# Last products of an inverse Fourier step: 128 channels as weights in two row halves instead of 64 in four quarters of the array

## The chip, the cores and the metric

The kernel runs on one core of one Trainium2 chip. The metric is the device time of one execution in microseconds (us). Three runs of the kernel before gave 2576.21, 2576.61 and 2581.67 us; the median, 2576.61 us, is the time before.

## What is computed

The reference filters each of 8 sequences of 3008 tokens and 256 channels in the frequency domain and passes the result through a two-layer network with SiLU. Everything is fp32.

```python
X = np.fft.rfft(x, axis=1)                       # x: 8 x 3008 x 256
Y = X * (filt_r + 1j * filt_i)[None]             # filters: 1505 x 256
y = np.fft.irfft(Y, n=3008, axis=1).reshape(24064, 256)
h = y @ w_in                                     # 256 x 2048
out = (h / (1 + np.exp(-h))) @ w_out             # 2048 x 256
```

## The kernel before

**The network.** The tokens are worked in 48 pairs of blocks (`PAIRS`, six for each sequence), and the 2048 hidden units in 8 steps for each pair, so there are 384 steps. Each step does 7 products for the hidden layer (`hidden`, line 758) and 7 for the output layer (`project`, line 821); seven rather than eight, because the 2 x 2 blocks are multiplied by a scheme that saves one product and pays with additions on VectorE. All of them use weights of 128 x 128 and 256 or 240 moving columns. The TensorE instructions of a step are written out one after the other by Python generators; `hidden` of one step and `project` of the step before are interleaved by rounds, 8 to a step.

**The Fourier part.** 3008 is split as 47 x 64. For each sequence `b`, `spectral(b)` does forward products, the multiplication with the filter and the inverse, and its pieces stand between the matmuls of the network steps of the sequence before. Where each piece goes is written by hand: `put(step, round, piece)`, `open_step` and `join` add it to the list `pending`, and `until` takes from it between rounds. The order of the instructions on every engine is therefore fixed in the program; no scheduler changes it. Sequence 0 has nothing to hide behind and is worked at the start, in the first 75 us.

**The last inverse products, `stage3(g)`, lines 576 to 602.** There are 8 groups `g` for each of 8 sequences, so 64 calls. A tile `t4` holds the values of 4 time residues `i` and 256 channels; its partitions 0 to 47 belong to half `h = 0` and 64 to 111 to half `h = 1` (48 rows: 24 frequency residues, real and imaginary parts). For each `h`, `i` and channel, the 48 values are multiplied with a constant table `wi_t` of 48 x 47, which gives 47 time points. In the instruction `t4` is the weights (`lhsT`, so the result has channels on its partitions) and `wi_t` streams as 47 moving columns. The two halves `h` use the upper and lower 64 rows of the array and write two PSUM banks, `ps[0]` and `ps[1]`, called `pd` in the profile. The channels come in blocks of 128 (`cb`), and each block in two parts of 64 (`c0`), which use the left and right 64 columns of the array. So four matmuls, two `c0` by two `h`, stand on four different quarters of the array. A call issues 2 (`cb`) x 4 (`i`) x 2 (`c0`) x 2 (`h`) = 32 matmuls. Each fp32 matmul appears in the profile as two weight loads and two matmul passes, so a call has 64 of each.

**Around it.** `load_t4` brings the `t4` tile of two groups later on SyncE's queue. After the products `evict_y` (line 608; line 602 for the first four calls) copies `ps[0]` and `ps[1]` into the tile `y` that the network reads, one copy on ScalarE and one on VectorE. A piece that has just `alone` uses the banks of `px` and `pyz`, one under `join` uses those of accumulators, so the products wait until the last reader of these banks is done. The first four calls (sequence 0, `g` 0 to 3) stand in the start phase beside VectorE's work that prepares the network's weights (lines 973 to 988).

Of the kernel before, what the change touches and what calls it, by code (L numbers as in the profile page):

```python
# [56 lines left out]
NS, NG = 24, 6  # L57
# [113 lines left out]
def kernel(  # L171
# [9 lines left out]
    nc = tc.nc  # L181
# [41 lines left out]
    wi_t = cpool.tile([128, N1], FP32)  # L223
# [27 lines left out]
    def bank(b, name, spare=None):  # L251


        if early[0] is None and spare in ("x", "yz"):
            return xps.tile([128, 2, C], FP32, name=name, tag=spare)
        if early[0] is None and spare is not None:
            return accps.tile([128, 2, C], FP32, name=name, tag=f"a{spare}")
        if early[0] is None:
            return fps.tile([128, 2, C], FP32, name=name, tag="f")
        early[0] += 1  # L260
        k = early[0] % 8
        if k < 2:
            return fps.tile([128, 2, C], FP32, name=name, tag="f")
        if k > 5:
            return xps.tile([128, 2, C], FP32, name=name, tag="x" if k == 6 else "yz")
        return accps.tile([128, 2, C], FP32, name=name, tag=f"a{k - 2}")

    def spectral(b):
# [295 lines left out]
        def load_t4(g):  # L564
            t4s[g] = t4pool.tile([128, 4, C], FP32, name=f"t4_{b}_{g}", tag="t4")
            for h in range(2):
                nc.sync.dma_start(out=t4s[g][64 * h:64 * h + 2 * NS], in_=d2[:, 4 * g:4 * g + 4, h, :])
# [8 lines left out]
        def stage3(g, home=None):  # L576

            half, n0 = divmod(4 * g, 16)
            ps = [bank(b, f"pd_{b}_{g}_{h}", home[h] if home else None)
                  .rearrange("p a c -> p (a c)")[:, 0:8 * N1]  # L580
                  .rearrange("p (a i n) -> p a i n", a=2, i=4) for h in range(2)]
            t4 = us["t4"][:, 4 * g:4 * g + 4] if b == 0 and g < 4 else t4s[g]
            for cb in range(2):
                for i in range(4):
                    for c0 in (0, 64):
                        for h in range(2):
                            rows = slice(64 * h, 64 * h + 2 * NS)
                            nc.tensor.matmul(  # L588
                                out=ps[h][c0:c0 + 64, cb, i, :],
                                lhsT=t4[rows, i, 128 * cb + c0:128 * cb + c0 + 64],  # L590
                                rhs=wi_t[rows, :], start=True, stop=True)
            if g < 6 and (b > 0 or g > 3):
                load_t4(g + 2)
            if n0 == 0:
                y[b, half] = ypool.tile([128, 2, HALF], FP32, name=f"y_{b}_{half}", tag="y")
            if early[0] is None:
                us["pd", g] = ps
                return
            dst = y[b, half].rearrange("p a (r h n) -> p a h r n", h=2, n=16)
            for h in range(2):  # L600
                copy = nc.vector.tensor_copy if g > 1 and h == 1 else nc.scalar.copy
                copy(out=dst[:, :, h, :, n0:n0 + 4], in_=ps[h].rearrange("p a i n -> p a n i"))  # L602

        def evict_y(g, h):
# [5 lines left out]
        return dict(us=us, store_rows=store_rows, evict_y=evict_y, evict_t1=evict_t1, halves=halves, load_first=load_first, stage1_first=stage1_first, fill_first=fill_first, load_x=load_x, load_two=load_two, sums=sums, stage1=stage1, reverse_x=reverse_x,  # L610
                    load_fold=load_fold, fold=fold, stage1_fold=stage1_fold, evict_fold=evict_fold,
                    load_t2=load_t2, forward=forward, multiply=multiply, add=add, inverse=inverse, inverse_first=inverse_first, rows_first=rows_first, even=even, rows=rows, load_t4=load_t4, load_t4_rows=load_t4_rows, stage3=stage3)

    pending = []
# [637 lines left out]
```

## Time and profile before

| what | value |
|---|---|
| median of 3 runs | 2576.61 us (2576.21 to 2581.67) |
| span of the profiled execution | 2574.2 us, 2.4 us less than the median of the runs |
| TensorE matmul (PE) | busy 2550.8 us (99%), 18810 passes |
| TensorE weight load (PEld) | busy 2195.8 us (85%), 18810 loads |
| VectorE (DVE), ScalarE (ACT), GpSimd (POOL) | 65%, 42%, 17% |
| mean granted TensorE clock | 0.997 |
| line 588, 60 calls after the start | 3840 passes, busy 67.2 us; 3840 loads, busy 61.2 us |
| line 588, the 4 calls in the start | 256 passes, busy 4.5 us; 256 loads, busy 4.2 us |

In the rows of the profile a group is given as line, engine, operation, output <- inputs, rows x columns of the array in use, shape of the operand, count; then the time in which at least one of the group was in flight, the mean duration of one, and the idle time before it. Passes and loads overlap in time, so a count times a mean is far more than the busy time. What a stage costs is read from the starts in the timeline, not from the means. A row of the timeline is a run of instructions of one line: its start, the time from the first start to the last end, and the number.

### The profile page before, as it was taken

What the parts mean: (1) busy time and instruction counts of PE and PEld (TensorE: products, weight loads), DVE (VectorE), ACT (ScalarE), POOL (GpSimd) and SP (SyncE); (2) the same over time, 40 slices, a digit from 0 to 9 for tenths busy, and PEclk for the clock granted to TensorE, in tenths of its full rate; (3) what the DMA queues carried; (4) which work ended last, traced back from release to release, by engine and by line L of the source; (5) the groups of instructions that cost most, each with busy time, mean ns of one, the idle gap of its engine ahead of it and who ended that gap; (6) DMA issues with size and microseconds to landing.
All of it is one profiled execution on the core that took longest, in us unless ns stands there. A gap on an engine that the chain in (4) does not pass through costs nothing.

```text
span 2574.2 us, 48031 instructions
## 1 busy us (share of the span) xinstructions
PE 2550.8 (99%) x18810; PEld 2195.8 (85%) x18810; DVE 1665.8 (65%) x3591; ACT 1086.3 (42%) x3009; POOL 429.1 (17%) x685
## 2 busy tenths in 40 slices
PE   8999999999999999999999999999999999999998
PEld 6688888888888888888888888888888888888987
DVE  7866666676666666666666676666666666555554
ACT  3544444444444444444444444444444444444443
POOL 3212111211121111311121111211121112101101
PEclk9999999999999999999999999999999999999999
DMA  9522232222222222322223122331232211200011
GB/s 290 160 60 53 78 70 64 60 73 67 59 64 68 73 67 50 82 70 67 58 73 78 48 67 63 76 79 46 66 85 67 67 42 33 60 18 16 9 17 17
DMA packets 199611, 171.08 MB, mean 66 GB/s; under 512 B 122068, under 2 KB 173380, under 8 KB 198500
## 3 DMA queue, kind: packets, MB, share of 16 engines
q1 hardware_dynamic: 178392, 117.06, 19.7%
q0 software_dynamic: 17344, 45.70, 5.6%
q10 hardware_dynamic: 3648, 5.24, 0.7%
q8 instruction: 148, 2.42, 0.4%
q14 instruction: 79, 0.65, 0.1%
HBM read 96.07 MB, written 81.26 MB: 69 GB/s over the span
## 4 chain that ended last, share of the span: by engine, by line
PE 96%; DMA 1%; DVE 1%; issue 0%; ACT 0%; POOL 0%; SPq 0%; DVEq 0%; ACTq 0%
PE acc L821 44%; PE px L758 26%; PE pyz L758 19%; PE pd L588 2%; PE pb L467 2%; PE pc L510 2%; PE pf L434 1%; PE pc L530 0%; DMA filt<-in_filt_i_dram 0%; PE pa L354 0%; DMA w_t<-in_x_dram 0%; PE pa L345 0%; DMA d_t<-d_tbl 0%; DVE w_t L988 0%; DMA raw<-in_moe_w_in_dram 0%
## 5 line engine op out<-in xcount | busy, mean ns | idle before, releaser
L821 PE MATMUL acc<-g,w_t 128*128 128x256 f32 (+1 forms) x5376 | 1510.2, 375 | 0.4 <-DVE g L729 0.4
L821 PEld LDWEIGHTS acc<-g,w_t 128*128 128x128 f32 x5376 | 1023.0, 190 | 114.4 <-DVE g L729 0.8
L729 DVE TENSOR_TENSOR g<-pyz,abc 128x256 f32<-128x256 f32 (+1 forms) x1152 | 480.1, 417 | 620.1 <-ACT abc L779 356.6
L729 DVE TENSOR_TENSOR g<-g 128x256 f32<-128x256 f32 (+3 forms) x1152 | 599.7, 521 | 196.7 <-ACT g L762 183.5
L758 PE MATMUL px<-ty,w_t 128*128 128x256 f32 (+1 forms) x2304 | 679.1, 376 | 1.8 <-ACT abc L773 1.2
L762 ACT ACTIVATE g<-g 128x256 f32<-128x256 f32 (+1 forms) x1152 | 472.9, 411 | 250.7 <-DVE g L729 250.7
L729 POOL TENSOR_TENSOR s<-s 128x256 f32<-128x256 f32 (+1 forms) x329 | 254.9, 792 | 1417.8 <-DVE s L841 1289.7
L758 PEld LDWEIGHTS px<-ty,w_t 128*128 128x128 f32 x2304 | 432.7, 190 | 65.3 <-issue 6.2
L758 PE MATMUL pyz<-y,w_t 128*128 128x256 f32 (+1 forms) x1536 | 454.1, 377 | 0.0
L758 PEld LDWEIGHTS pyz<-y,w_t 128*128 128x128 f32 x1536 | 283.8, 190 | 47.6 <-DVE g L729 7.7
L773 ACT COPY abc<-px 128x256 f32<-128x256 f32 (+1 forms) x384 | 141.2, 368 | 372.7 <-PE px L758 372.7
L779 ACT COPY abc<-px 128x256 f32<-128x256 f32 (+1 forms) x384 | 141.5, 368 | 338.1 <-PE px L758 337.1
L762 ACT ACTIVATE g<-px 128x256 f32<-128x256 f32 (+1 forms) x384 | 145.8, 380 | 300.9 <-PE px L758 300.7
L758 PE MATMUL px<-y,w_t 128*128 128x256 f32 (+1 forms) x768 | 232.3, 384 | 1.0 <-DVE y L602 1.0
L758 PE MATMUL pyz<-ty,w_t 128*128 128x256 f32 (+1 forms) x768 | 225.4, 375 | 0.2 <-DVE g L729 0.2
L758 PEld LDWEIGHTS px<-y,w_t 128*128 128x128 f32 x768 | 140.5, 190 | 32.9 <-DVE y L608 5.8
L758 PEld LDWEIGHTS pyz<-ty,w_t 128*128 128x128 f32 x768 | 144.5, 190 | 18.7 <-DVE g L729 1.0
L766 ACT COPY abc<-px 128x256 f32<-128x256 f32 (+1 forms) x384 | 135.3, 352 | 52.3 <-PE px L758 52.3
L588 PEld LDWEIGHTS pd<-wi_t,t 48*64 48x64 f32 x3840 | 61.2, 135 | 25.3 <-ACT g L762 16.4
L446 POOL DMA_DIRECT2D d<-tf x144 | 71.6, 504 | 29.5 <-DVE tf L442 29.5
L871 DVE STREAM_TRANSPOSE o<-s 128x256 f32<-128x256 f32 x192 | 74.0, 423 | 0.4 <-issue 0.4
L841 ACT COPY s<-acc 128x512 f32<-128x512 f32 (+1 forms) x94 | 54.2, 577 | 47.6 <-PE acc L821 47.3
(137 smaller groups left out, 1264.4 us busy)
## 6 DMA issues: line engine op xcount, KB each, us to landing
t<-d SPq DMA_DIRECT2D x120, 192.0 KB
t<-d SPq DMA_DIRECT2D x84, 256.0 KB
d<-q POOLq DMA_DIRECT2D x84, 256.0 KB, 2.7
out_dram<-o SPq DMA_DIRECT2D x636, 32.0 KB
d<-tf POOLq DMA_DIRECT2D x144, 96.0 KB, 3.5
xr<-in_x_dram SPq DMA_DIRECT2D x6, 1472.0 KB
x_all<-in_x_dram SPq DMA_DIRECT2D x72, 96.0 KB
x_all<-xr SPq DMA_DIRECT2D x72, 96.0 KB
```

Source lines behind the costliest of these rows:

```text
L446: nc.gpsimd.dma_start(out=d1[k // 2, :, k % 2, n0:n0 + 4], in_=us["tf"][32 * k:32 * k + NS].rearrange("p q n c -> p (q n) c"))
L467: nc.tensor.matmul(out=ps[k][32 * j:32 * j + 32, ri, :], lhsT=d_t[rows, 4 * g + at, ri, :], rhs=rhs, start=True, stop=True)
L588: nc.tensor.matmul(out=ps[h][c0:c0 + 64, cb, i, :], lhsT=t4[rows, i, 128 * cb + c0:128 * cb + c0 + 64], rhs=wi_t[rows, :], start=True, sto ...
L729: eng.tensor_tensor(out=out, in0=in0, in1=in1, op=op)
L758: nc.tensor.matmul(out=out, lhsT=w_t[:, jp, c, 0], rhs=rhs, start=start, stop=True, skip_group_check=True)
L762: nc.scalar.activation(out=g[:, k, 0:n], in_=g[:, k, 0:n] if src is None else src, func=AFT.Silu)
L766: nc.scalar.copy(out=sums[:, 0, 0:n], in_=xo)
L773: nc.scalar.copy(out=sums[:, 1, 0:n], in_=xo)
L779: nc.scalar.copy(out=sums[:, 2, 0:n], in_=xo)
L821: nc.tensor.matmul(out=acc[pair][i][:, h, 0:n], lhsT=w_t[:, jp, c, 1], rhs=g[:, k, 0:n], start=(jp == 0 and h == 0), stop=last, skip_group ...
L841: copy(out=s[:, 2 * i:2 * i + 2, 0:n], in_=acc[pair][i][:, :, 0:n])
L871: v.transpose(out=o[:, :, h, :], in_=results[pair][:, ((2, 6), (4, 1))[chunk][h], :])
```

## The change

The loop over `c0` goes away. Each matmul takes a whole block of 128 channels as its weights and writes 128 partitions of PSUM; the halves `h` stay on the upper and lower rows of the array. A call issues 16 matmuls instead of 32, so 32 passes and 32 loads instead of 64 and 64, two at a time instead of four. The moving operand (47 columns of `wi_t`), the banks, the results and their places are the same. In the built program the waits stand on the same places (the first matmul of each half), and the instruction order on every engine is otherwise unchanged.

```diff
             for cb in range(2):
                 for i in range(4):
-                    for c0 in (0, 64):
-                        for h in range(2):
-                            rows = slice(64 * h, 64 * h + 2 * NS)
-                            nc.tensor.matmul(
-                                out=ps[h][c0:c0 + 64, cb, i, :],
-                                lhsT=t4[rows, i, 128 * cb + c0:128 * cb + c0 + 64],
-                                rhs=wi_t[rows, :], start=True, stop=True)
+                    for h in range(2):
+                        rows = slice(64 * h, 64 * h + 2 * NS)
+                        nc.tensor.matmul(out=ps[h][:, cb, i, :], lhsT=t4[rows, i, 128 * cb:128 * cb + 128],
+                                         rhs=wi_t[rows, :], start=True, stop=True)
```

## The prediction, made before the changed kernel ran

> **What bounds the kernel now.** I read the page's first part (busy times) and its fourth (the chain that ended last) before anything else.
>
> ```profile
> PE 2550.8 (99%) x18810; PEld 2195.8 (85%) x18810; DVE 1665.8 (65%) x3591; ACT 1086.3 (42%) x3009; POOL 429.1 (17%) x685
> ...
> PE 96%; DMA 1%; DVE 1%; issue 0%; ACT 0%; POOL 0%; SPq 0%; DVEq 0%; ACTq 0%
> ```
>
> TensorE is busy for 99% of the span and 96% of the chain is its work. So a stage of TensorE that gets longer or shorter moves the end by the same amount, unless TensorE waits soon after it for something else. The view of waits, asked for TensorE's matmuls alone, lists fourteen waits of together about 14 us in 2574, nearly all of them before 85 us. From 85 us on there is next to nothing that could swallow added time.
>
> Next, the groups of weight loads, different shapes kept apart; the last two numbers that matter are the mean duration of one load (after the comma) and, before it, the busy time.
>
> ```profile
> L821 PEld LDWEIGHTS acc<-g,w_t 128*128 128x128 f32 x5376 | 1023.0, 190 | 114.4 <-DVE g L729 0.8
> ...
> L588 PEld LDWEIGHTS pd<-wi_t,t 48*64 48x64 f32 x3840 | 61.2, 135 | 25.3 <-ACT g L762 16.4 <-issue 8.5 <-DVE g L729 0.4
> L510 PEld LDWEIGHTS pc<-z,e_t 32*64 32x64 f32 x1344 | 28.3, 131 | 10.6 <-PE acc L821 6.8
> L467 PEld LDWEIGHTS pb<-t,d_t 64*32 64x32 f32 x1344 | 20.5, 106 | 15.4 <-issue 7.1 <-PE px L758 2.3
> ```
>
> A load's duration goes with its columns (128: 190 ns, 64: 131 to 135, 32: 106), about 0.9 ns for each, and hardly with its rows (32 or 48 rows, 131 or 135). From 64 to 128 columns it is 55 ns. That is a latency; what a load keeps others waiting is read from starts. Here is the timeline of the loads around one call of the changed stage, and then around two calls in a row.
>
> ```profile
> 152.74 0.41 PEld L821 LDWEIGHTS acc<-g,w_t 128*128 128x128 f32 x2
> 153.48 1.02 PEld L588 LDWEIGHTS pd<-wi_t,t 48*64 48x64 f32 x64 [0.33 <-issue]
> 154.56 0.30 PEld L758 LDWEIGHTS px<-ty,w_t 128*128 128x128 f32 x2
> 154.88 0.41 PEld L821 LDWEIGHTS acc<-g,w_t 128*128 128x128 f32 x2
> ```
>
> ```profile
> 335.26 1.96 PEld L588 LDWEIGHTS pd<-wi_t,t 48*64 48x64 f32 x128 [0.33 <-issue]
> 337.27 0.30 PEld L758 LDWEIGHTS px<-y,w_t 128*128 128x128 f32 x2
> ```
>
> Three readings. **(1) The pace now.** 128 loads are 32 rounds of four quarters. From the first start to the last end it is 1.96 us; less the last load (0.135) and the three starts inside a round (0.02), 31 rounds take 1.805 us, so 58 ns for a round. A call of 16 rounds is 0.93 us. **(2) What sets that pace.** The first two 128-column loads after the stage stand in 0.30 us: the second starts 0.30 - 0.19 = 0.11 us after the first, with no matmul to wait for. In the steady rows two loads stand in 0.41 us, so 0.22 us apart; there the 256 moving columns set the pace (0.84 ns a column). In the changed stage the stream of 47 columns would need only 47 x 0.84 = 39 ns, and a load plus its stream, one after the other, 53 + 39 = 92 ns (53 ns being half of the 0.107 us that 128 columns need). The measured 58 ns is neither; it is the load of 64 columns and some 5 ns. So the loads bound this stage, and each load goes on beside the stream of the matmul before it. **(3) Four at once.** All four loads of a round fit into those 58 ns, so different quarters are loaded at the same time.
>
> The warm-up loop at the start gives the pace of 128-column loads under a short stream, from the timeline of loads:
>
> ```profile
> 8.94 1.53 PEld L1051 LDWEIGHTS idle<-wx_t 96*128 96x128 f32 x13
> ```
>
> (1.53 - 0.19) / 12 = 0.112 us a load. Here the stream has 128 columns too, so load and stream are equal, and the row is an upper bound for a 128-column load under 47 columns; the 0.11 above, a pair with nothing between, agrees from the other side.
>
> **The change part by part.** It removes 32 of 64 loads and 32 of 64 passes from each of 64 calls. It adds 64 columns to each load left. The number of rounds stays 16: before, a round was 4 quarters by 64 columns; after, 2 row halves by 128 columns. Only the length of a round changes.
>
> *The 60 calls after the start.* A round goes from 58 ns to that of a 128-column load, 0.112 us (warm-up row). 16 x (0.1115 - 0.058) = 0.856 us for a call, and 60 x 0.856 = 51.4 us. No work of another engine hides it: the page's PE row is full before and after, and what follows (`px`, `acc`) waits for the same engine.
>
> *The 4 calls in the start.* Here VectorE prepares weights beside TensorE, and TensorE has a hole:
>
> ```profile
> 69.78 1.54 PE L588 MATMUL pd<-wi_t,w_t 48*64 48x47 f32 x89
> 72.30 1.83 PE L588 MATMUL pd<-wi_t,w_t 48*64 48x47 f32 x108 [0.98 <-issue]
> ```
>
> The hole of 0.98 us is put down to "issue", no semaphore. The instruction queue of the page moved 2.42 MB for 37620 TensorE records, 64 bytes each; I take the hole for instructions that come too late at this dense place (an inference). With half the records in longer time it should go. Then the four calls end at 68.65 (first start) + 0.27 (extra in the first call, whose second half starts late) + 64 x 0.1115 + 0.17 (end of a pass) = 76.2 us instead of 74.13. After them stand VectorE's second copy of `y` (L602, 0.54 us, ended at 74.97 on the chain) and the `ty` sums that the network waits for. VectorE was free at 74.05, so these now come some 0.2 us after 76.0, and I take +1.8 us. If the hole stays it is +2.8.
>
> *One more hole* of 0.3 us of the same kind (a run of 93 passes of L588 takes 1.93 us at 1605.67, where two calls otherwise need 2.08 for 128) would go: -0.3 us.
>
> *Entering and leaving the stage.* Before the stage the loads stand idle for 0.33 us (0.03 in steady rows, 0.22 less 0.19), and after it the next full load starts 0.16 us after the last pass started. Whether a 64 x 128 division of the array is entered and left at the same price no row shows: there is no such shape in the trace. From above: 0.1 us more at each of 47 runs of calls (60 calls in 46 runs, one at the start), 5 us. From below: nothing is lost at all, the first load being pulled under the stream before as in steady rows, which is worth up to 0.15 us at the entry and 0.2 at the exit, 0.35 x 47 = -16 us. I take 0, as every division in the trace (64 x 64, 64 x 32, 32 x 64, 32 x 32) shows idle time at its borders.
>
> *What does not change.* Copies, DMAs and waits keep their number and order; the copies of 128 x 376 (0.47 on ACT, 0.55 on DVE) start 0.86 us later, as does the `t4` load two groups ahead. They follow TensorE and move with it.
>
> Sum: 51.4 + 1.8 - 0.3 = +52.9 us. On the profiled span 2574.2 + 52.9 = 2627.1; the runs' median lies 2.4 us over the span, so **2629.5 us** (+2.1%).
>
> Two rules of the Trainium skill are weighed here. "TensorEngine Tiling (Array Packing)", Restrictions, says that dividing the array by columns switches fast weight load off, which speaks against this forecast: without column division a 128-column load could be quick. "TensorE: Matmul & The Clock Gate", Weight-path perf modes, leaves fp32 out of fast weight load, and this trace's undivided fp32 loads do take 0.11 us. By the first rule alone the loads would vanish behind the stream and the time would be about that of the faster rival below; I go by the row. The same page, Part 3, says that a load overlaps running matmuls only on different row groups; by it each round would be load plus stream, the third rival below. The steady rows contradict it: loads of all 128 rows 0.22 us apart, no longer than their stream.
>
> **Rivals.**
>
> *Faster.* If a 128-column load in a 64-row half took no more than the stream, a round would be 39 + 5 = 44 ns, and 16 x 64 x (0.044 - 0.058) = -14 us: 2562 us. It begins to be faster as soon as the new load takes under 58 ns in the 64-row half. For it: half as many instructions, and no row of just this shape. Against it: 0.11 us for every 128-column load seen, whatever its rows (96 or 128). 5%.
>
> *The halves load one after the other.* Then a call is 32 x 0.1115 = 3.57 us, +2.64, and 64 calls give +169 us: 2745. For it: no row shows two 128-column loads side by side. Against it: now four loads, two of them on the same rows, run at once. 6%.
>
> *Load and stream do not overlap in a row half.* A round is 0.1115 + 0.039 = 0.151 us, a call +1.49, together +95 us: 2671. Against it: the 58 ns of today's round. 4%.
>
> *No change.* The added 53 us would have to lie in waits that TensorE has anyway; the waits listed are 14 us, most of them at the start. 3%.
>
> **How the numbers follow.** Forecast as above: 82%, with its own range from 2629.5 - 16 (free borders) - 5 (waits after a call, of DVE and ACT, that become shorter), 2608, to 2629.5 + 5 (dearer borders) + 1 (hole stays) + 5 (spread of the runs before), 2640. That range holds 8 in 10, so the other cases stay outside. Within 0.2% is about what a measurement of this kernel tells from no change. Faster 5%, same 3%, slower 92% (82 + 6 + 4).
>
> **What the profile after will show.** Line 587 has 32 loads of 48 x 128 for each call; a lone call's loads stand in about 15 x 0.1115 + 0.19 = 1.87 us instead of 1.02, two calls in 3.66 instead of 1.96; mean of a load about 190 ns. Loads of the two halves start some 7 ns apart. TensorE's records fall by 2048 of each kind, to 16762. The waits list stays as short. I am wrong if the rounds come at another pace than 0.11 us, if the loads' idle time before the stage is not 0.33 us, or if waits of TensorE behind the stage shrink by microseconds.

## The result, and the profile after

The changed kernel takes 2649.16 us (median of 4 runs, 2648.34 to 2650.91) against 2579.1 us of the kernel before in the same series: ratio 1.0279, 95% interval 1.0267 to 1.0291, so +70 us where the forecast was +53 and its range ended at 2640. The profiled execution has a span of 2649.0 us, 74.8 more than the one before; it is the longest of its four, and the one before was near the shortest of its own, so the bill of the two profiles below is some 5 us over the difference of the medians.

The first part of the page of the changed kernel, its row of granted clock (40 slices of the span) and the shares of the chain, then the same clock row of the kernel before:

```profile
PE 2624.4 (99%) x16762; PEld 2263.4 (85%) x16762; DVE 1658.8 (63%) x3591; ACT 1086.3 (41%) x3009; POOL 425.9 (16%) x685
...
PEclk9899999999999999999999999999999999999999
...
PE 95%; DMA 2%; DVE 1%; ACT 0%; issue 0%; ACTq 0%; SPq 0%; DVEq 0%
```

```profile
PEclk9999999999999999999999999999999999999999
```

TensorE is as full as before, with 2048 fewer passes and 2048 fewer loads. One digit of the clock row has fallen to 8, and the mean granted clock from 0.997 to 0.989. A share that small is easy to pass over. But 0.8% of 2649 us that were not granted are some 21 us of full-speed work, most of which TensorE still had to do.

Now the stage itself, in the timeline of loads: one call alone, then two in a row. A row gives start, length from the first start to the last end, and what.

```profile
163.01 0.41 PEld L818 LDWEIGHTS acc<-g,w_t 128*128 128x128 f32 x2
163.75 1.86 PEld L587 LDWEIGHTS pd<-wi_t,t 48*128 48x128 f32 x32 [0.33 <-issue]
165.67 0.30 PEld L755 LDWEIGHTS px<-ty,w_t 128*128 128x128 f32 x2
...
348.89 3.65 PEld L587 LDWEIGHTS pd<-wi_t,t 48*128 48x128 f32 x64 [0.33 <-issue]
352.60 0.30 PEld L755 LDWEIGHTS px<-y,w_t 128*128 128x128 f32 x2
```

A call alone went from 1.02 to 1.86 us and a pair from 1.96 to 3.65: 0.84 us more for each call. The idle time before it is 0.33 us as before, and the gap behind its last load 0.06 us in both kernels. So 60 x 0.84 = 50.4 us lie in the loads. The other 24 of the 74.8 us lie elsewhere. Here is what TensorE does behind that pair:

```profile
348.90 3.77 PE L587 MATMUL pd<-wi_t,t 48*128 48x47 f32 x64
352.60 0.91 PE L755 MATMUL px<-y,w_t 128*128 128x256 f32 x2
353.30 1.06 PE L755 MATMUL pyz<-y,w_t 128*128 128x256 f32 x2
354.16 1.06 PE L818 MATMUL acc<-g,w_t 128*128 128x256 f32 x2
...
356.55 0.59 PE L818 MATMUL acc<-g,w_t 128*128 128x256 f32 x2
```

Two passes of 256 columns take 0.59 us in the last row and 1.06 in the rows above: their starts stand 0.43 us apart instead of 0.22. TensorE waits for nothing there; it runs at half speed. The granted clock in stretches of 3.4 us says so (time, busy time and count of each engine, then the clock as PEclk). The last row is the stretch around the end of the same pair in the kernel before:

```profile
core 0: us, PE busy (x) PEld busy (x) DVE busy (x) ACT busy (x) POOL busy (x), PEclk, DMA share, GB/s
346.20:349.60 3.40, 3.40 (x27) 2.79 (x25) 2.60 (x5) 1.26 (x4) 0.00 (x0) 1.00 0.00 0
349.60:353.00 3.40, 3.40 (x58) 3.32 (x57) 0.69 (x2) 0.47 (x1) 0.00 (x0) 0.99 0.26 74
353.00:356.40 3.40, 3.40 (x10) 2.68 (x9) 1.87 (x5) 0.66 (x3) 0.00 (x0) 0.51 0.91 163
356.40:359.80 3.40, 3.40 (x18) 2.99 (x17) 2.81 (x7) 1.83 (x6) 0.00 (x0) 1.00 0.00 0
```

```profile
336.10:339.50 3.40, 3.40 (x98) 3.05 (x89) 1.52 (x5) 1.04 (x3) 0.00 (x0) 1.00 0.54 130
```

"PE busy" is 3.40 of 3.40 in all of them and tells nothing; the count of passes and the clock tell it. Between the start and the last product the trace has nine such stretches (3.41 us each, two of them joined), every one in or just behind one of the 14 pairs; six pairs have none. The kernel before has none from 84 us to its last product, which ends at 2565 us. All halved stretches of a run begin on one grid of 3.41 us, whose phase differs from run to run.

The four calls of the start run at half clock all but 0.2 us (the clock is low from 69.7 to 93.5 us; in the kernel before it was full while they ran and low for one stretch, from 80.3 us):

```profile
69.44 0.43 PE L587 MATMUL pd<-wi_t,w_t 48*128 48x47 f32 x2 [4.40 <-DVE w_t L972]
70.33 13.85 PE L587 MATMUL pd<-wi_t,w_t 48*128 48x47 f32 x126 [0.47 <-DMA w_t<-d]
```

13.85 us for 126 passes, 63 rounds, is 0.22 us a round, twice 0.11. The first call after the start begins at 163.8 us, before the change at 153.5. The bill of the two profiled executions is then: start +10.3; 60 calls x 0.84 = +50.4; the rest, 74.8 - 10.3 - 50.4 = 14.1, for nine halved stretches, 1.6 us each (that this rest belongs to them is what the experiments test). A stretch of 3.41 us at half speed loses 1.7 us of work at most.

### The profile page after: what moved, and what is told of

The parts are those of the page before. It is cut to its first block, busy times and chain, and to the rows that moved or that the text cites. A ratio compares the mean times of both kernels' runs of the same rounds, so it can differ in the third digit from the quotient of the medians.

```text
span 2649.0 us, 43935 instructions
## 1 busy us (share of the span) xinstructions
PE 2624.4 (99%) x16762; PEld 2263.4 (85%) x16762; DVE 1658.8 (63%) x3591; ACT 1086.3 (41%) x3009; POOL 425.9 (16%) x685
## 4 chain that ended last, share of the span: by engine, by line
PE 95%; DMA 2%; DVE 1%; ACT 0%; issue 0%; ACTq 0%; SPq 0%; DVEq 0%
PE acc L818 42%; PE px L755 25%; PE pyz L755 18%; PE pd L587 5%; PE pb L467 2%; PE pc L510 2%; PE pf L434 1%; DMA raw<-in_moe_w_out_dram 0%; DMA w_t<-in_x_dram 0%; PE pa L354 0%; DMA filt<-in_filt_r_dram 0%; DVE g L726 0%; DMA w_t<-d 0%; DMA d_t<-d_tbl 0%; DMA raw<-in_moe_w_in_dram 0%
## 5 line engine op out<-in xcount | busy, mean ns | idle before, releaser
L726 DVE TENSOR_TENSOR g<-g 128x256 f32<-128x256 f32 (+3 forms) x1152 | 592.1, 514 | 196.7 <-ACT g L759 183.6
L763 ACT COPY abc<-px 128x256 f32<-128x256 f32 (+1 forms) x384 | 135.3, 352 | 80.3 <-PE px L755 80.3
L587 PEld LDWEIGHTS pd<-wi_t,t 48*128 48x128 f32 x1920 | 112.2, 189 | 24.9 <-ACT g L759 16.4
L587 PE MATMUL pd<-wi_t,t 48*128 48x47 f32 x1920 | 118.1, 287 | 0.2 <-DVE g L726 0.2
L605 DVE COPY y<-pd 128x376 f32<-128x376 f32 x60 | 32.9, 549 | 75.4 <-PE pd L587 75.4
```

Of the source, the lines that this page charges most:

```text
L587: nc.tensor.matmul(out=ps[h][:, cb, i, :], lhsT=t4[rows, i, 128 * cb:128 * cb + 128], rhs=wi_t[rows, :], start=True, stop=True)
L605: copy(out=dst[:, :, h, :, n0:n0 + 4], in_=us["pd", g][h].rearrange("p a i n -> p a n i"))
L726: eng.tensor_tensor(out=out, in0=in0, in1=in1, op=op)
L763: nc.scalar.copy(out=sums[:, 0, 0:n], in_=xo)
```

## Experiments

**The clock theory**: the loads cost 0.84 us a call, and everything beyond comes from the granted clock, which halves when the streams of matmuls fill less than about half of a 3.41 us stretch. **Rivals**: the whole loss is loads and borders, spread over all calls; or the clock falls for a reason of its own, such as waits in the start. Of each profiled execution two numbers help: where the first call after the start begins (the first start of `pd` from a `t4` tile), and what the rest of the span is. These two and the count of halved stretches (up to the last product) come from one profiled execution of each kernel, the ratio from all its runs.

| run | ratio to before (95%) | first call after the start, us | rest of the span, against 2420.7 | of this 0.84 x wide calls | halved stretches after the start |
|---|---|---|---|---|---|
| before | 1 | 153.5 | 0 | 0 | 0 |
| the change | 1.0279 (1.0267 to 1.0291) | 163.8 | +64.5 | 50.4 | 9 |
| e1 lone calls wide | 1.0106 (1.0091 to 1.0121) | 155.9 | +27.2 | 26.9 | 0 |
| e2 pairs wide | 1.0143 (1.0126 to 1.0160) | 155.3 | +33.4 | 23.5 | 6 |
| e3 start wide | 1.0028 (1.0018 to 1.0038) | 162.8 | 0.0 | 0 | 0 |
| e4 64 columns, zeros | 1.0230 (1.0206 to 1.0254) | 166.2 | +57.4 | 50.4 | 4 |
| e5 pairs pulled apart | 1.0202 (1.0187 to 1.0218) | 155.8 | +53.8 | 50.4 | 0 |
| e6 both halves in one | 1.0157 (1.0138 to 1.0176) | 152.1 | +41.5 | | 0 |
| e7 64 columns, data | 1.0223 (1.0202 to 1.0245) | 159.3 | +54.9 | 50.4 | 3 |
| e8 eighths | 1.0295 (1.0278 to 1.0312) | 163.1 | +74.3 | | 14 |
| e9 changed, more filler | 1.0277 (1.0259 to 1.0294) | 163.6 | +62.8 | 50.4 | 8 |
| e10 before, more filler | 1.0004 (0.9995 to 1.0014) | 157.5 | +0.2 | 0 | 0 |

### e1, e2, e3: the change in three parts

```diff
-                    for c0 in (0, 64):
+                    n_c = 128 if wide_call else 64
+                    for c0 in range(0, 128, n_c):
...
```

The products below take `n_c` channels. `wide_call` is `g > 3` in e1 (32 lone calls), `b > 0 and g < 4` in e2 (28 calls, 14 pairs), `b == 0 and g < 4` in e3 (the four of the start).

> 128 channels as weights only in the 32 calls that stand alone between other work (g from 4 on); the pairs and the four calls of the start stay in quarters. Clock theory (a call costs 0.84 us more because its rounds are bound by the loads; everything beyond that comes from the granted clock, which falls to half when a stretch of 3.41 us on a fixed grid has matmul streams in less than about half of it): a lone call is 1.9 us, too short to empty a stretch, so 32 x 0.84 = +27 us, ratio 1.0105, clock as before (0.997). Rival, loads and borders only (the whole loss spread evenly over the 64 calls, 70 / 64 = 1.1 us each): +35 us, ratio 1.0136.

> 128 channels as weights only in the 28 calls that stand two in a row (14 pairs). Clock theory: 28 x 0.84 = 23.5 us, plus about 8 of the 14 pairs that halve the clock for one or two stretches at some 1.7 us each, so +30 to +45 us, likeliest +37, ratio 1.0145, several half-clock stretches that begin at the end of a pair. Rival, loads and borders only: 28 x 1.1 = +31 us and no half-clock stretch after the start.

> 128 channels as weights only in the four calls of the start. Clock theory: the calls run at half clock and can't bring it back, since at half clock too their streams fill only some 37% of a stretch; about +10 us, ratio 1.004, the clock low until the network's products have run for a while. Rival, loads only, as in my forecast: 4 x 0.85 less the hole of 1 us, +1.8 us, ratio 1.0007.

e1 came out at 1.0106: after the start +27.2 us for 32 calls, 0.85 each, and no halved stretch. e2 came out at 1.0143: 23.5 us of loads and 9.9 for six halved stretches (I had expected about eight). The same kind of call costs 0.85 us alone and 1.19 in a pair, so a loss spread evenly over the calls has fallen. One of e2's pairs and the stretch behind it:

```profile
359.80:363.20 3.40, 3.40 (x64) 3.40 (x64) 0.99 (x2) 1.55 (x3) 3.24 (x5) 1.00 0.09 25
363.20:366.60 3.40, 3.40 (x14) 2.87 (x11) 0.83 (x2) 0.73 (x2) 2.56 (x5) 0.50 0.81 213
366.60:370.00 3.40, 3.40 (x19) 3.19 (x18) 1.51 (x5) 1.02 (x3) 0.00 (x0) 1.00 0.84 260
```

In the first row loads go on without a break (3.40 of 3.40), so the clock did not fall through an engine with nothing in flight; it fell after a stretch full of loads with short streams.

e3 lies between the two expectations: 1.0028 is +7 us, not 10 and not 1.8, and its nine runs spread from 2579.52 to 2589.27. After the start nothing is left (0.0). The three ratios less one add up to 0.0277, the whole change is 0.0279.

### e4, e7: longer streams under the same loads

```diff
-    wi_t = cpool.tile([128, N1], FP32)
+    wi_t = cpool.tile([128, 64], FP32)
...
+    nc.gpsimd.memset(wi_t[:, N1:64], 0.0)
```

e7 loads 17 columns of the table there instead. The PSUM view has 64 columns for each `i`; the copies read 47 of them.

> As the changed kernel, but the table has 64 columns instead of 47 (the last 17 are zeros, and their results are not read), so a round is still bound by the load of 128 columns (0.112 us) while the streams fill 53 ns of it instead of 39. Clock theory: the stretches of the pairs rise from 0.40 to 0.48 of stream to above half, so no halving after the start; 60 x 0.84 = 50 us and 2 to 5 for the start, +54 us, ratio 1.021, clock 0.996. Rival, loads and borders only: no change against the changed kernel, ratio 1.027 to 1.029, or slower through the longer streams.

> As the run with 64 columns, but the 17 added columns hold values of the table instead of zeros. If what counts for the clock is the time of streams (near half of a stretch): as with zeros, ratio 1.021 to 1.025, about four halved stretches after the start. If zeros don't count as work: hardly any halved stretch after the start, ratio 1.021 or less, clock 0.995 to 0.997.

Both lie below the changed kernel, and the work after the start falls from +64.5 to +57.4 and +54.9 with four and three halved stretches instead of nine. (The profile of e4 is of its slowest run, 2646 us against a median of 2635.) So longer streams help although each round does more, as the clock theory has it; but my guess that 64 columns suffice was wrong. Zeros or data make no difference that these two runs can tell (their intervals overlap).

The guess failed at "about half". A stretch wholly inside a pair has 30 rounds, and by the stream of one half they fill 30 x 39 ns = 35% of it in the changed kernel and 30 x 53 ns = 47% here. But the expectation's 0.40 to 0.48 fits another count, the time in which either half streams (the two start 7 ns apart). An estimate of that share, from the starts of all matmuls in the traces at 0.84 ns a column, for the stretches after the start: in the changed kernel 41 to 47% lost the clock and one of 49% kept it; in e4 stretches of 51 to 54% and in e7 of 53% lost it. So no single share of streaming time divides them. Weighted with the part of the array that a product uses (48 x 128 of 128 x 128 for one half), the three runs agree better: the clock was lost up to 0.36, 0.38 and 0.38 and kept from 0.37, 0.40 and 0.38. e8 below does not fit that either (0.26 lost, 0.21 kept). That short streams under long loads lower the clock is shown by the runs; what exactly it counts stays open.

### e5: the pairs pulled apart

On the changed kernel, with the four calls of the start in quarters:

```diff
-        open_step(at - 10, *alone(part, 0), (part["stage3"], 1))
+        alone_at(at - 11, 3, part, 0)
+        open_step(at - 10, (part["stage3"], 1))
...
-        join(at - 8, part, 2, 3)
+        join(at - 8, part, 2)
+        alone_at(at - 6, 3, part, 3)
```

> 128 channels as weights in all 60 calls after the start, but the second call of each pair is moved some 1.4 or 1.3 steps away from the first, so that none stand together; the four calls of the start stay in quarters. Clock theory: no stretch after the start is emptied, so the clock is as before (0.997) and the loads alone are left: 60 x 0.84 = 50 us and 14 x 0.34 = 5 us for the borders of the calls pulled apart, +55 us, ratio 1.0214. Rival (the clock falls through something else in the changed kernel, or the loss beyond 0.84 us a call is not the clock): ratio as with the pairs together, 1.0106 and 1.0143 added, 1.025, and half-clock stretches left after the start.

1.0202, and no halved stretch from 87 us to the last product. The mean granted clock of its four runs is 0.996 to 0.998, as before (0.995 to 0.996 in the same series), where e2 has 0.990 to 0.992. Two calls pulled apart, each with the stretch behind it:

```profile
336.40:339.80 3.40, 3.40 (x40) 2.91 (x39) 0.73 (x3) 0.84 (x3) 0.00 (x0) 1.00 0.00 0
339.80:343.20 3.40, 3.40 (x20) 2.73 (x18) 2.30 (x5) 1.69 (x5) 0.00 (x0) 1.00 0.50 116
343.20:346.60 3.40, 3.40 (x40) 3.15 (x40) 1.09 (x3) 0.37 (x1) 0.00 (x0) 1.00 0.11 32
346.60:350.00 3.40, 3.40 (x17) 2.87 (x16) 3.30 (x9) 1.84 (x6) 0.00 (x0) 1.00 0.39 89
```

All 60 calls are wide here and the after-start loss is 53.8 us: 50.4 of loads and 3.4 for 14 more borders (0.24 each, where I had 0.34). So with 47 columns the wide form halves the clock after the start only where two calls stand together. A lone one fills its stretch, by the stream of one half, with 16 x 39 ns and about 1.2 us of network products, some 53% (an estimate), and was never followed by a halving here.

### e6: both halves in one product over 96 rows

```diff
-                    for h in range(2):
-                        rows = slice(64 * h, 64 * h + 2 * NS)
-                        nc.tensor.matmul(out=ps[h][:, cb, i, :], lhsT=t4[rows, i, 128 * cb:128 * cb + 128],
-                                         rhs=wi_t[rows, :], start=True, stop=True)
+                    nc.tensor.matmul(out=ps[cb][:, i], lhsT=t4[0:96, i, 128 * cb:128 * cb + 128],
+                                     rhs=wi_t, start=True, stop=True)
...
```

The table becomes 96 x 94, the second half of `t4` is loaded from partition 48 on instead of 64, and the copies read the banks in the new order.

> The two halves h as one product: 96 rows (48 and 48), 128 channels as weights, and a table of 96 x 94 with the two small tables on its diagonal. A call is 8 matmuls, so 16 loads of 128 columns one after the other instead of 16 rounds of two; streams of 94 columns; no division of the array, so no borders. Clock theory with loads as the bound: a call is 16 x 0.112 = 1.79 us with nothing at its borders, against 1.275 for a lone call and 1.10 for one of a pair before: 32 x 0.51 + 28 x 0.69 = +36 us, and about +3 in the start (streams of 78 ns in 112 hold the clock): +39, ratio 1.015, clock 0.996. If borders cost as much without the division: +55, ratio 1.021. Rival (loads do not matter, the loss is the clock and the division): near the kernel before, ratio 1.00 to 1.005.

1.0157, where 1.015 was expected from 0.112 us a load. The two parts did not come out as well as the sum: +41.5 us after the start for the expected 36, and the first call after the start 1.4 us earlier instead of about 3 later. Around a lone call, loads:

```profile
151.66 0.41 PEld L821 LDWEIGHTS acc<-g,w_t 128*128 128x128 f32 x2
152.09 1.97 PEld L590 LDWEIGHTS pd<-wi_t,t 96*128 96x128 f32 x16
153.98 0.30 PEld L758 LDWEIGHTS px<-ty,w_t 128*128 128x128 f32 x2
```

The 0.33 us of idle time before the stage is gone, the array being undivided; the first load lies under the stream before. 16 loads in a row take as long as 16 rounds of two in the changed kernel (1.97 against 1.86 us, of which 0.1 is the first load's wait for that stream). So the two halves' loads in the changed kernel do run beside each other, and the loads are the bound; the rival "loads do not matter" has fallen. The table's empty corners cost nothing: streams of 94 columns (78 ns of 112, 70%) hold the clock, and there is no halved stretch from 56 us to the last product. This version is 1.2% faster than the changed kernel and 1.6% slower than the kernel before.

### e8: the other direction, eighths

```diff
-                    for c0 in (0, 64):
+                    for c0 in (0, 32, 64, 96):
```

with 32 columns for each product.

> The other direction: 32 channels as weights, eight matmuls at a time on eighths of the array; 128 loads and 128 passes for a call. If today's 58 ns are the load of 64 columns alone, a load of 32 takes 27 ns, the stream of 39 + 5 = 44 ns becomes the bound, and 16 x 64 x (0.044 - 0.058) = -14 us, ratio 0.9945. If the records themselves set a pace (starts inside a round now stand 6.6 ns apart), a round of 16 records is at least 0.106 us: 16 x 64 x (0.106 - 0.058) = +49 us, ratio 1.019, and more where instructions come late.

Neither. A call that goes undisturbed takes 1.24 us, so a round is (1.24 - 0.106 - 0.06) / 15 = 72 ns: more than the 58 of quarters, though its loads are half as long, and less than the 106 I took for 16 records. But 25 times there is a hole. First the waits of its matmuls (line, what it waited for, us in total, times, longest), then a stretch of its timeline with the second of two calls in a row:

```profile
PE pd L588 <- issue: 41.9, 25, 2.5
```

```profile
346.29 1.59 PE L588 MATMUL pd<-wi_t,t 48*32 48x47 f32 x145
350.01 0.65 PE L588 MATMUL pd<-wi_t,t 48*32 48x47 f32 x46 [2.13 <-issue]
```

Twice the records bring holes of up to 2.5 us put down to no semaphore, 42 us in all, and all 14 halved stretches after the start follow such a hole. In the kernel before there were two (1.0 and 0.3 us), in the changed kernel there is none on this line. That goes with instructions which come too late where they are dense; no run here shows it directly.

### e9, e10: the wait ahead of the start's calls filled

```diff
-    idle_wide(16)
+    idle_wide(26)
```

e9 on the changed kernel, e10 on the kernel before.

> The changed kernel with ten more filler products (20 passes, 4.3 us at full clock) between the forward work and the four calls of the start, where TensorE otherwise waits some 4.4 us for data. If the low clock of the start comes from that wait alone, the four calls now run at full clock: 5 to 8 us less than the changed kernel, ratio 1.0255. If the calls themselves empty the stretches (streams of 39 ns in 112, four calls in a row, 7.2 us), the clock falls within the calls all the same, a stretch or two later: 0 to 3 us less, ratio 1.027.

> The kernel before with the same ten filler products more. Its calls in quarters fill 39 of 58 ns with streams and hold the clock if they get it at full speed: the stretch or two of half clock seen in the start of the runs with quarters (10 us in two of them) go, 0 to 3 us less, ratio 0.999 to 1.000; if the filler delays the calls instead, up to 2 us more, ratio 1.0008.

e9 is no faster than the changed kernel (1.0277). The filler removed the wait, the four calls began at 72.97 us with the full clock, and lost it while they ran:

```profile
68.00:72.00 4.00, 4.00 (x20) 3.53 (x19) 3.93 (x9) 0.87 (x2) 0.00 (x0) 1.00 0.40 119
72.00:76.00 4.00, 4.00 (x59) 3.60 (x59) 2.08 (x5) 0.85 (x2) 1.61 (x4) 1.00 0.09 18
76.00:80.00 4.00, 4.00 (x48) 4.00 (x46) 0.00 (x0) 0.85 (x2) 2.72 (x6) 0.57 0.64 175
80.00:84.00 4.00, 3.61 (x34) 3.45 (x34) 0.87 (x2) 0.84 (x2) 0.00 (x0) 0.50 0.01 5
```

So the wait is not needed for the fall: the calls bring it about themselves, and at half clock, with loads and streams both twice as long, their share of streams is the same and did not bring the clock back. e10 gains nothing (interval across 1), against its expectation: its calls in quarters had two short waits as they began and ran at half clock in that profile:

```profile
70.29 7.10 PE L588 MATMUL pd<-wi_t,w_t 48*64 48x47 f32 x254 [0.72 <-DMA w_t<-d]
```

```profile
70.40:73.80 3.40, 3.40 (x131) 3.40 (x133) 3.33 (x8) 0.85 (x2) 0.20 (x1) 0.50 0.13 44
73.80:77.20 3.40, 3.40 (x133) 3.40 (x127) 0.56 (x2) 1.32 (x3) 2.96 (x7) 0.50 0.40 89
```

At half clock as at full, a round in quarters streams for two thirds of its time (39 of 58 ns, 67%; here both are twice as long). That went on through two whole stretches, and the clock still did not come back until 87.4 us, while quarters that began at full clock kept it in the kernel before (68.7 to 74.1 us). So to bring the clock back took more than to keep it. The start's clock and waits differ between executions of one kernel (first call after the start at 153.5 to 157.5 us in quarters, 159.3 to 166.2 wide), so the start's share of the change is known to some 5 us only.

## Why the prediction failed

*"A round goes from 58 ns to that of a 128-column load"* was right: 0.84 us a call against 0.856, by the rows of one call and of two, and by e1 (0.85) and e5. *The two halves load at once* was right (e6). *The borders keep their price* was right: 0.33 us before and 0.06 us behind, in both kernels. *No work hides it* was right: the waits of TensorE after the start, about 1 us in all, stayed. *The hole of the start goes* was right. The faster rival and the two slower ones (2671 and 2745) needed another round than 0.112 us; none came. None of the signs of being wrong that the prediction listed (another pace, another idle time at the border, shorter waits) appeared, and it was wrong all the same: the clock was not among them.

What failed is the step *"Only the length of a round changes"*. I divided 39 ns of stream by 58 ns of round to find the bound, and did not divide it by 112: the streams' share of the stage fell from 67% to 35%, and the granted clock depends on it. I had the mean clock, 0.997, and no term for it. It was worth 14.1 us after the start (nine halved stretches) and, as far as two profiles can tell, most of the start's +10.3, where I had put +1.8 for the calls at full clock. Together with 50.4 this is the measured difference; the forecast had 51.4 + 1.8 - 0.3. e5, which takes the halving after the start away and leaves the loads, measured +52 us (ratio 1.0202). That this is nearly the forecast is in part luck: it has 3.4 us of added borders, and the start in quarters.

The Trainium skill has a mechanism that fits, on the page "TensorE: Matmul & The Clock Gate", Part 1: the clock is gated by how busy TensorE was in a window of about 3.4 us that runs freely, and its two states are half and full. These runs agree: stretches of 3.41 us and multiples, a clock of 0.50 or 1.00, one grid a run. In its section on why this matters for kernels the page warns of idle gaps of TensorE longer than about 3 us. Here no gap was needed: loads filled 3.40 of 3.40 us, and the clock fell. In this case pairs (35% by the stream of one half) lost the clock at 8 of 14 places, pairs padded to 47% at 4 and 3 of 14, and lone wide calls (53%, estimated above) nowhere. That is a rule of thumb for these calls; by the estimates under e4 and e7 streaming time alone is not what is counted, and the count stays open.

That pairs fall in some sequences and not in others goes with the phase of the grid: a pair of 3.65 us only just covers a stretch of 3.41, so most stretches hold network products too. In e2 the halvings recur every 317.4 us, 93 stretches, at the same pair of each sequence. That this is locking (a halving delays the work by its own loss and so keeps the next pair in phase) is an inference; no run tested it.

## What to carry over

Ahead of a change to small matmuls, work out two quotients for a stage: load time over round time, which gives the pace, and stream time over round time, which warns of the clock. In this kernel a stage with the second under about a half for longer than 3.4 us lost some 1.6 us for each stretch of half clock behind it (8 of 14 pairs had one or two), and a longer one stayed at half clock to its end; breaking the stage up or giving it longer streams helped. Here loads paid by their columns as soon as they were longer than the streams, so splitting weights by columns over the array (four quarters at once, 58 ns a round) beat the wide form with half the instructions (112 ns); eight at once (72 ns and 42 us of holes) did not.

## What was not expected of the hardware

- Weight loads did not hold the clock: with loads in flight for all of 3.40 us and streams of one half in some 35% of it the granted clock fell to 0.50 for the next 3.41 us (e2).
- Keeping the clock and bringing it back are different: calls in quarters kept a full clock in the kernel before, but at half clock two whole stretches of them (67% streams) did not bring it back (e10).
- At half clock a load of 128 columns lasts 327 ns instead of 189 on average, so a stage bound by loads also takes twice as long, and its share of streams cannot rise:

```profile
L587 PEld LDWEIGHTS pd<-wi_t,t 48*128 48x128 f32 x1920 | 112.2, 189 | 24.9 <-ACT g L759 16.4 <-issue 8.3 <-DVE g L726 0.3
...
L587 PEld LDWEIGHTS pd<-wi_t,w_t 48*128 48x128 f32 x128 | 14.0, 327 | 5.4 <-DVE w_t L972 4.8 <-ACT e L957 0.6
```

- Rounds of eight products of 32 columns take 72 ns, more than rounds of four of 64 (58 ns), though each load is shorter (106 against 135 ns).
